# Keeping the pieces of the next batch's transform out of every third slot of a GEGLU block (batches 3 to 7)

## The chip, the cores and the metric

The kernel runs on one core of one Trainium2 chip. The metric is the time of one execution on the device in microseconds (us). The time before is 620.68 us, the median of six runs between 619.86 and 621.28 us.

## The reference, cut to what matters

```
x: (8, 3008, 256)                                  # batch, sequence, channels
X   = real(fft(fft(x, axis=1), axis=2))            # Fourier mixing
X   = X.reshape(24064, 256)
g   = X @ w_gate                                   # 256 -> 1536
val = X @ w_val                                    # 256 -> 1536
out = (gelu(g) * val) @ w_out                      # 1536 -> 256, float32
```

## The kernel before, in words

**The transform.** The Fourier transform of one batch is made of matmuls. GpSimd first folds the input (sums and differences of a row and its mirror, lines 221 to 229) into `eo`. Eight pieces `s1t` (line 546) then multiply it by a table `G` in two or three matmuls each, and ScalarE copies each result to `S_sb` (line 558). Two DMA writes (`z_write`, line 562) put `S_sb` into DRAM, one DMA (`z_read`, line 571) brings it back in another layout as `Z_sb`, 768 KB. Seven more pieces follow: `tp_row` (line 621), one matmul that makes a row which a DMA writes to DRAM at once, and `tp_e` and `tp_o` (line 584) for each of three groups, four matmuls of up to 128 columns each, copied by ScalarE into `E_sb` and `O_sb` (line 601). Last, `tp_rows` (line 638) is two DMAs that spread the row. The transform of the real input has a mirror symmetry, so only about half of the tokens is held, as an even part E and an odd part O. A token and its mirror come out of E plus O and E minus O.

**The feed-forward block.** Each batch has three chunks of 512, 512 and 481 columns of E and O, and each chunk has 12 slices of the 1536 hidden features. One slice of one chunk is a *slot*: 36 slots a batch, 288 in all, numbered here from 0. In slot i TensorE does the following, in this order (`feed`, lines 981 to 1000): the gate of slice i (two matmuls into a `ps_g` bank), the mirrored gate of slice i-1 (one more matmul into the bank of that slice), the first value matmul of slice i, four matmuls of the second layer, the second value matmul of slice i-1, four more matmuls of the second layer, and then whatever the table `fill` has for this slot. ScalarE applies gelu to the gate (line 690) and to the mirrored gate (line 699). VectorE does three operations a slot on the value (lines 718, 734, 736), GpSimd one (line 738). The second layer works on the chunk before.

**Evacuation.** The second layer sums 128 tokens and their mirrors in one `ps_o` bank over six pieces of four matmuls. With two pieces in a slot a bank is complete at the end of every third slot, the slots with number 2 modulo 3. There ScalarE copies it to `out_sb` (line 783), and four DMAs store it (line 668), issued by SyncE (SP).

**Buffers.** PSUM has two `ps_g` banks, three `ps_v`, one `ps_o` and two `ps_dft` for the transform pieces. A `ps_g` bank is filled at the start of slot i, gets its mirrored part in slot i+1, is released by that part's gelu (line 699), and is filled again at the start of slot i+2.

**The order.** Each engine runs its instructions in program order, and the program order is written by hand: `plan` (line 889) builds the tables `fill` (pieces, loads and DMAs of the transform) and `pool` (the folding on GpSimd), keyed by slot, and `feed` empties them slot by slot. The transform of batch b runs in the slots of batch b-1. Its `s1t` pieces begin up to nine slots ahead of that batch and are placed from line 949 on. The function `spread` (line 920) places the seven later pieces evenly between two slots, and `taken` holds the slots that it used. What `fill` has for a slot comes behind the slot's evacuation in program order, on SP too: the DMAs of a `fill` entry in a slot with an evacuation are issued after that evacuation's stores.

Of the kernel before, what the change touches and what calls it, by code (L numbers as in the profile page):

```python
# [18 lines left out]
def _sub(base: bass.AP, free_pattern, free_offset, part_start=0, part_num=None):  # L19
    p_step, p_count = base.ap[0]  # L20
    if part_num is None:
        part_num = p_count - part_start
    pat = [[p_step, part_num]] + [list(x) for x in free_pattern]
    off = base.offset + part_start * p_step + free_offset
    return ap_replace(base, ap=pat, offset=off)
# [3 lines left out]
def kernel(  # L29
# [80 lines left out]
    def S_tile():  # L110
        return work([96, 16, C], BF16, "A", 1, "S_sb")
# [33 lines left out]
    def psum(tag):  # L145
        bufs = {"g": 2, "v": 3, "o": 1, "dft": 2}[tag]
        return psum_pool.tile([128, 512], FP32, tag=tag, bufs=bufs, name=f"ps_{tag}")
# [287 lines left out]
    def load_wo(q):  # L435
        n = NFC // 2
        nc.gpsimd.dma_start(
            out=Wo_sb[:, q * n : (q + 1) * n, :],
            in_=ap_replace(
                moe_w_out, ap=[[C, 128], [128 * C, n], [1, C]], offset=moe_w_out.offset + q * n * 128 * C))  # L440
# [61 lines left out]
    def state(b):  # L502
        return dst_.setdefault(b, {})
# [20 lines left out]
    def ch(b, pp, engine="A", qs=(0, 1)):  # L524

        def run():
            st = state(b)
            A = st["A"]
            if "Z" not in st:
                st["Z"] = Z_tile()  # L530
            ps = ps_any(b)
            for i, q in enumerate(qs):
                k = 2 * (2 * pp + q)
                for g in range(2):
                    nc.tensor.matmul(  # L535
                        ps[:, i * C : (i + 1) * C], _sub(A, [[1, 128]], g * NK * K1 + k * K1), II[:, g, :, :],
                        start=g == 0, stop=g == 1)
            n = len(qs) * C
            dst = _sub(st["Z"], [[1, n]], pp * 512 + qs[0] * C)
            if engine == "A":  # L540
                nc.scalar.activation(dst, ps[:, :n], AF.Copy)
            else:
                nc.vector.tensor_copy(dst, ps[:, :n])
        return run

    def s1t(b, jg, half):

        def run():
            st = state(b)
            if "S" not in st:  # L550
                st["S"] = S_tile()
            ps = psum("dft")
            for q, js in enumerate(JG[jg][2 * half : 2 * half + 2]):
                for j in js:
                    nc.tensor.matmul(  # L555
                        ps[:96, q * C : (q + 1) * C], G[:, j, :], _sub(eo, [[1, C]], j * C),
                        start=(j == js[0]), stop=(j == js[-1]))
            nc.scalar.activation(  # L558
                _sub(st["S"], [[1, 512]], (4 * jg + 2 * half) * C, part_num=96), ps[:96, :], AF.Copy)
        return run  # L560
# [23 lines left out]
    def tp_e(b, gi, g=0, engine="A", tag=None):  # L584
        def run():
            st = state(b)
            if b not in EO_bufs:
                EO_bufs[b] = EO_tiles()
            ps = psum(tag) if tag else ps_any(b)
            for pair, o, n in pairs(gi):  # L590
                nc.tensor.matmul(  # L591
                    ps[:, o : o + n], st["Z"][:, pair, g * 128 : g * 128 + 128], _sub(TP, [[1, n]], g * 128),
                    start=True, stop=True)
            if b == 0 and g == 1:
                for pair, o, n in pairs(gi):
                    nc.tensor.matmul(
                        ps[0:1, o : o + n], st["Z"][:, pair, 128:129], _sub(TP, [[1, n]], 0), start=True, stop=True)
            n = chunk_len[gi]
            dst = _sub(EO_bufs[b][g], [[1, n]], chunk_off[gi])
            if engine == "A":  # L600
                nc.scalar.activation(dst, ps[:, :n], AF.Copy)  # L601
            else:
                nc.vector.tensor_copy(dst, ps[:, :n])
        return run
# [42 lines left out]
    def tp_o(b, gi, engine="A"):  # L647
        return tp_e(b, gi, 1, engine)
# [238 lines left out]
    NS = NG * NFC  # L887

    def plan():

        fill, pool = {}, {}

        def at(table, s, f):
            table.setdefault(s, []).append(f)

        early = []
        for gi in (1, 2):
            e = "A" if gi == 1 else "V"
            early += [ch(0, 2 * gi), ch(0, 2 * gi + 1, e), tp_e(0, gi), tp_o(0, gi, e), tp_y(0, gi)]
        for s, f in (  # L900
                (0, make_w(0, 256, 256, m_engine="P")), (0, make_w(1, 256, 256, engine="V", m_engine="P")),
                (1, make_w(1, 512, 512, (1,), m_engine="P")), (1, lambda: load_wo(0)), (1, lambda: load_wo(1)),
                (2, make_w(0, 512, 512, (0,), "V")), (3, make_w(0, 512, 512, (1,))), (3, make_w(1, 512, 512, (0,), "V")),
                (4, make_w(1, 1024, 512, (1,), "V")), (5, make_w(0, 1024, 512, (0,), "V")),
                (5, make_yw()), (6, make_w(0, 1024, 512, (1,))), (6, tp_y(0, 0)), (7, make_w(1, 1024, 512, (0,), "V"))):
            at(fill, s, f)
        for i, f in enumerate(early):
            at(fill, (7, 8, 9, 10, 11, 12, 13, 14, 15, 16)[i], f)


        at(fill, 7, lambda: nc.sync.dma_start(
            out=ap_replace(yrow_dram[0], ap=[[0, 1], [1, 64]]), in_=EB_bufs[0][0:1, 0:64]))
        for k, s in ((0, 8), (1, 9), (2, 9)):
            at(fill, s, lambda k=k: load_part(2, k, (load_forward,)))
        for k, s in ((0, 18), (1, 19), (2, 19)):
            at(fill, s, lambda k=k: load_part(2, k, (load_mirror,)))

        taken = set()

        def spread(b, s0, s1):  # L920

            items = [tp_row(b)] + [f(b, gi) for gi in range(NG) for f in (tp_e, tp_o)]
            for i, f in enumerate(items):
                s = s0 + (i * (s1 - s0) // (len(items) - 1) if b > 1 else (0, 2, 3, 6, 8, 11, 13)[i])
                at(fill, s, f)
                taken.add(s)
                if b == 1 and i and i % 2 == 0:
                    at(fill, s + 1, tp_rows(b, chunk_off[i // 2 - 1], chunk_len[i // 2 - 1]))
            if b > 1:
                at(fill, s + 1, tp_rows(b, 0, HALF))  # L930

        for b in range(1, B):
            s0 = (b - 1) * NS
            ops = []
            for j0, nj in PIECES:
                ops += fold_ops(b, j0, nj, nc.gpsimd)
            per = len(ops) // 5
            first, n = (s0 - 19, 30) if b == 3 else (s0 - 22, 32)
            slot_of = [first + i * n // len(ops) for i in range(len(ops))]
            if b == 2:  # L940
                slot_of = [26, 27, 29, 30, 31, 33, 34, 37, 38, 39, 41, 42, 43, 45, 46, 49, 50, 50, 51, 51]
            if b == 1:
                slot_of = [4, 4, 5, 5, 6, 6, 7, 7, 8, 8, 9, 13, 13, 14, 15, 15, 16, 17, 17, 18]
            for s, f in zip(slot_of, ops):
                at(pool, s, f)
            if 1 < b < B - 1:
                for k, piece in ((0, 1), (1, 3), (2, 4)):
                    at(fill, slot_of[piece * per + 1] + 1, lambda b=b, k=k: load_part(b + 1, k))
            s = s0 - 9 if b > 1 else 12
            for i, (jg, piece) in enumerate(((2, 1), (1, 2), (0, 3), (3, 4))):  # L950
                ready = slot_of[piece * per + per - 1] + 2
                for g in range(2):
                    s = max(s + 1, ready)
                    while s in taken:
                        s += 1
                    at(fill, s, s1t(b, jg, g))
                if i == 2:
                    at(fill, s + 1, z_write(b, 0, 12))
                if i == 3:
                    at(fill, s + 1, z_write(b, 12, 4))  # L960
            at(fill, s + 2, z_read(b))
            if b == 1:
                spread(b, s + 7, s + 20)
                continue
            assert s + 7 < s0 + NS - 10
            spread(b, s + 7, s0 + NS - 5 if b == 2 else s0 + NS - 6)
        return fill, pool

# [70 lines left out]
```

## Time and profile before

| what | value |
|---|---|
| median of six runs | 620.68 us |
| the profiled execution, its own time | 620.76 us |
| its span in the trace | 618.9 us |
| TensorE weight loads busy | 406.6 us (66%) |
| VectorE busy | 576.5 us (93%) |
| ScalarE busy | 425.1 us (69%) |
| GpSimd busy | 508.8 us (82%) |
| ScalarE gelu, line 690 / line 699 | 288 at 589 ns / 288 at 586 ns |
| ScalarE evacuation, line 783 | 92 at 598 ns |
| ScalarE copy of an `s1t` piece, line 558 | 56 at 589 ns |
| ScalarE copy of a `tp_e` or `tp_o` piece, line 601 | 45 at 588 to 589 ns |
| granted TensorE clock, mean | 0.997 |

[...]Two instructions that follow each other on one engine overlap by about 0.1 us in the records, so the spacing of their starts tells the cost in a busy queue better than the duration. The ends of matmuls are modelled, but their starts are recorded.

### The profile page before, as it was taken

To read this page: it belongs to the slowest core of one execution; us is meant where nothing else is said; L and a number is where in the kernel's file an instruction comes from. 1 tells how busy PE (TensorE), PEld (TensorE's weight loads), DVE (VectorE), ACT (ScalarE), POOL (GpSimd) and SP (SyncE) were. 2 spreads that over 40 slices of the span, in tenths; PEclk is the share of its full clock that TensorE was granted. 3 is DMA by queue.
4 is the path that set the end of the run, shared out by engine and by line. 5 is a ranking of instruction groups with operands and counts; after the bars stand their busy time and mean duration, and the time that the engine had idled before them with its cause. 6 is when DMAs were issued, how large, how long until landed. Compare 5 with 4: busy or idle time off the path is not lost.

```text
span 618.9 us, 12794 instructions
## 1 busy us (share of the span) xinstructions
PE 610.6 (99%) x4230; PEld 406.6 (66%) x4230; DVE 576.5 (93%) x940; ACT 425.1 (69%) x825; POOL 508.8 (82%) x513
## 2 busy tenths in 40 slices
PE   8999999999999999999999999999999999999997
PEld 4456666666666666666666666666666666666666
DVE  8789999999999999999999999999999999999992
ACT  6787677677766676666767677666776667666651
POOL 8889899999997999879997899969987555555561
PEclk8999999999999999999999999999999999999999
DMA  9961825546362364632553335543123322221123
GB/s 173 200 136 34 237 69 154 135 120 183 85 170 79 94 150 111 156 96 55 160 139 101 112 97 117 140 107 95 44 69 77 95 56 51 64 50 43 40 52 82
DMA packets 52466, 65.40 MB, mean 106 GB/s; under 512 B 7629, under 2 KB 47278, under 8 KB 50004
## 3 DMA queue, kind: packets, MB, share of 16 engines
q1 hardware_dynamic: 45472, 49.03, 30.4%
q0 software_dynamic: 6608, 15.29, 11.5%
q8 instruction: 33, 0.54, 0.4%
q10 hardware_dynamic: 320, 0.26, 0.2%
q14 instruction: 33, 0.27, 0.1%
HBM read 39.65 MB, written 30.17 MB: 113 GB/s over the span
## 4 chain that ended last, share of the span: by engine, by line
PE 95%; DMA 2%; DVE 1%; ACT 1%; issue 1%; POOL 0%; POOLq 0%; SPq 0%; ACTq 0%; DVEq 0%
PE ps_o L763 39%; PE ps_g L674 30%; PE ps_v L674 20%; PE ps_dft L555 2%; PE ps_dft L591 2%; DMA xb<-in_x_dram,idx 1%; DMA out_dram<-out_sb 1%; PE ps_dft L451 1%; PE ps_o L832 0%; ACT A_sb L519 0%; PE ps_dft L535 0%; DVE h_sb L730 0%; DVE W_sb L459 0%; POOLq L1034 0%; POOL h_sb L738 0%
## 5 line engine op out<-in xcount | busy, mean ns | idle before, releaser
L738 POOL TENSOR_TENSOR h_sb<-gelu_sb,v_sb 128x512 bf16<-128x512 bf16 (+1 forms) x280 | 319.7, 1146 | 90.8 <-DVE v_sb L736 77.4
L763 PE MATMUL ps_o<-Wo_sb,h_sb 128*128 128x256 bf16 (+1 forms) x2232 | 334.5, 273 | 0.0
L763 PEld LDWEIGHTS <-h_sb 128*128 128x128 bf16 (+1 forms) x2304 | 228.7, 100 | 111.1 <-POOL h_sb L738 1.2
L690 ACT ACTIVATE gelu_sb<-ps_g 128x512 bf16<-128x512 f32 (+1 forms) x288 | 169.5, 589 | 99.3 <-PE ps_g L674 93.1
L718 DVE SCALAR_TENSOR_TENSOR ve_sb<-EB_sb,yw,ps_v 128x512 f32<-128x512 bf16 (+1 forms) x280 | 206.2, 737 | 20.6 <-PE ps_v L674 16.6
L674 PEld LDWEIGHTS <-W_sb 128*128 128x128 bf16 x1440 | 138.1, 98 | 81.2 <-issue 3.6
L734 DVE TENSOR_TENSOR h_sb<-gelu_sb,ps_v 128x512 bf16<-128x512 bf16 (+1 forms) x280 | 189.8, 678 | 1.4 <-ACT gelu_sb L699 1.0
L736 DVE SCALAR_TENSOR_TENSOR v_sb<-ve_sb,ps_v 128x512 f32<-128x512 f32 (+1 forms) x280 | 187.4, 669 | 0.0
L674 PE MATMUL ps_g<-O_sb,W_sb 128*128 128x512 bf16 (+1 forms) x576 | 168.9, 374 | 0.1
L699 ACT ACTIVATE gelu_sb<-ps_g 128x512 bf16<-128x512 f32 (+1 forms) x288 | 168.8, 586 | 0.0
L674 PE MATMUL ps_v<-E_sb,W_sb 128*128 128x512 bf16 (+1 forms) x288 | 108.0, 375 | 0.7 <-DVE W_sb L459 0.6
L674 PE MATMUL ps_g<-E_sb,W_sb 128*128 128x512 bf16 (+1 forms) x288 | 108.0, 375 | 0.7 <-ACT gelu_sb L699 0.3
L674 PE MATMUL ps_v<-O_sb,W_sb 128*128 128x512 bf16 (+1 forms) x288 | 108.0, 375 | 0.0
L783 ACT ACTIVATE out_sb<-ps_o 128x512 f32<-128x512 f32 x92 | 55.0, 598 | 34.3 <-PE ps_o L763 34.0
L229 POOL TENSOR_TENSOR eo_sb<-ab_sb 94x512 bf16<-94x512 f32 (+1 forms) x70 | 77.7, 1111 | 0.4
L558 ACT ACTIVATE S_sb<-ps_dft 96x512 bf16<-96x512 f32 x56 | 33.0, 589 | 18.7 <-PE ps_dft L555 18.2
L225 POOL TENSOR_TENSOR ab_sb<-x_raw,x_raw 94x508 f32<-94x508 f32 (+1 forms) x30 | 33.0, 1099 | 0.0
L222 POOL TENSOR_TENSOR ab_sb<-x_raw,x_raw 94x508 f32<-94x508 f32 (+1 forms) x30 | 33.0, 1099 | 0.0
L555 PE MATMUL ps_dft<-eo_sb,G 94*96 94x256 bf16 x119 | 22.3, 272 | 0.0
L601 ACT ACTIVATE E_sb<-ps_dft 128x512 bf16<-128x512 f32 (+1 forms) x23 | 13.5, 588 | 8.9 <-PE ps_dft L591 8.9
L163 POOL DMA_INDIRECT x_raw<-in_x_dram,idx x18 | 17.2, 957 | 2.9 <-issue 0.8
L601 ACT ACTIVATE O_sb<-ps_dft 128x512 bf16<-128x512 f32 (+1 forms) x22 | 13.0, 589 | 7.5 <-PE ps_dft L591 7.0
(151 smaller groups left out, 208.2 us busy)
## 6 DMA issues: line engine op xcount, KB each, us to landing
out_dram<-out_sb SPq DMA_DIRECT2D x364, 64.0 KB
x_raw<-in_x_dram SPq DMA_DIRECT2D x10, 768.0 KB
Z_sb<-z SPq DMA_DIRECT2D x7, 768.0 KB
z<-S_sb SPq DMA_DIRECT2D x7, 576.0 KB
EB_sb<-yrow SPq DMA_DIRECT2D x6, 376.2 KB
z<-S_sb SPq DMA_DIRECT2D x7, 192.0 KB
x_raw<-in_x_dram SPq DMA_DIRECT2D x2, 640.0 KB
x_stage<-in_x_dram SPq DMA_DIRECT2D x1, 768.0 KB
```

Source lines behind the costliest of these rows:

```text
L222: eng.tensor_tensor(ab(0, 1, up), fwd(1, up), mir(255, down), op=ALU.add)
L229: eng.tensor_tensor(_sub(eo, [[C, nj], [1, 128]], j0 * C + g * 128), ab(0, 0, [[1, 128]]), ab(1, 0, [[1, 128]]), op=op)
L555: nc.tensor.matmul(ps[:96, q * C : (q + 1) * C], G[:, j, :], _sub(eo, [[1, C]], j * C), start=(j == js[0]), stop=(j == js[-1]))
L674: nc.tensor.matmul(ps[:, :n], W[nm, part][:, fs], src, start=start, stop=stop, **kw)
L690: nc.scalar.activation(gl[:, 0, :n], pg[:, :n], AF.Gelu)
L699: nc.scalar.activation(_sub(gl, [[-1, n]], TOK + n - 1), pg[:, :n], AF.Gelu)
L718: nc.vector.scalar_tensor_tensor(ve[:, :n], EB_bufs[b][:, c0 : c0 + n], yw[:, fc : fc + 1], pv[:, :n], op0=ALU.mult, op1=ALU.add)
L734: nc.vector.tensor_tensor(st["h"][:, fc, 0, :n], gl[:, 0, :n], pv[:, :n], op=ALU.mult)
L736: nc.vector.scalar_tensor_tensor(_sub(vv, [[-1, n]], n - 1), ve[:, :n], 2.0, pv[:, :n], op0=ALU.mult, op1=ALU.subtract)
L738: nc.gpsimd.tensor_tensor(st["h"][:, fc, 1, :n], gl[:, 1, :n], vv[:, :n], op=ALU.mult)
L763: nc.tensor.matmul(pso[:m, half], st["h"][:, fc, sign, h0 : h0 + m], Wo_sb[:, fc, :], start=(fc == 0 and not (first and sign)), stop=(fc = ...
L783: nc.scalar.activation(_sub(osb, [[1, 2 * C]], 0, part_num=m), pso[:m, :], AF.Copy)
```

## The change

A new function `quiet` moves a slot number up until the slot has no transform piece yet and isn't 2 modulo 3. From batch 3 on it places all pieces: the eight `s1t`, and the seven of `spread`, which no longer spaces them evenly but takes the next such slot for each. Batches 1 and 2 keep their places. What is placed relative to a piece (`z_write`, `z_read`, `tp_rows`) goes with it. The bound of the assertion is eased by two slots.

```diff
         taken = set()
 
+        def quiet(s):
+
+            while s in taken or s % 3 == 2:
+                s += 1
+            taken.add(s)
+            return s
+
         def spread(b, s0, s1):
 
             items = [tp_row(b)] + [f(b, gi) for gi in range(NG) for f in (tp_e, tp_o)]
             for i, f in enumerate(items):
-                s = s0 + (i * (s1 - s0) // (len(items) - 1) if b > 1 else (0, 2, 3, 6, 8, 11, 13)[i])
+                if b > 2:
+                    s0 = s = quiet(s0)
+                else:
+                    s = s0 + (i * (s1 - s0) // (len(items) - 1) if b > 1 else (0, 2, 3, 6, 8, 11, 13)[i])
                 at(fill, s, f)
                 taken.add(s)
...
                 for g in range(2):
                     s = max(s + 1, ready)
-                    while s in taken:
+                    while b == 2 and s in taken:
                         s += 1
+                    s = quiet(s) if b > 2 else s
                     at(fill, s, s1t(b, jg, g))
...
-            assert s + 7 < s0 + NS - 10
+            assert s + 7 < s0 + NS - 8
             spread(b, s + 7, s0 + NS - 5 if b == 2 else s0 + NS - 6)
```

Worked out from the code, the pieces of batch 4 and of the start of batch 5 stand in these slots (batches 5 to 7 are like them, 36 slots apart; an E marks a slot with an evacuation):

| piece | before | after |
|---|---|---|
| `s1t` 1 to 4 of batch 4 | 101E, 103, 105, 106 | 103, 105, 106, 108 |
| `s1t` 5, 6; first `z_write` | 112, 113E; 114 | 112, 114; 115 |
| `s1t` 7, 8; second `z_write` | 118, 119E; 120 | 118, 120; 121 |
| `z_read` | 121 | 122E |
| `tp_row` | 126 | 127 |
| `tp_e`, `tp_o` in turn | 128E, 130, 132, 134E, 136, 138 | 129, 130, 132, 133, 135, 136 |
| `tp_rows` | 139 | 137E |
| `s1t` 1 to 4 of batch 5 | 137E, 139, 141, 142 | 138, 139, 141, 142 |

## The prediction

> **What bounds the kernel now.** I read the busy shares first, then the chain that ended last, then the waits.
>
> ```profile
> PE 610.6 (99%) x4230; PEld 406.6 (66%) x4230; DVE 576.5 (93%) x940; ACT 425.1 (69%) x825; POOL 508.8 (82%) x513
> PE 95%; DMA 2%; DVE 1%; ACT 1%; issue 1%; POOL 0%; POOLq 0%; SPq 0%; ACTq 0%; DVEq 0%
> ```
>
> TensorE is busy for 99% and makes 95% of the chain. The ends of matmuls are modelled, so 99% could hide small waits. I therefore measured slots in the timeline, from the start of a slot's first gate matmul to the next slot's. Slots without a transform piece take 1.95 us with chunks of 512 (316.03 to 317.98) and 1.89 us with 481 (306.07 to 307.96). A 512-column matmul starts 0.21 to 0.22 us before its follower, a 256-column one 0.11 us: 5 x 0.215 + 8 x 0.11 = 1.95. So the plain slot is nothing but matmuls. VectorE, at 93%, isn't the bound: its line 718 starts 0.40 to 0.42 us behind its value matmul in nearly every slot, so it follows and has no backlog.
>
> The list of waits from 36 to 600 us (total, times, longest) shows what TensorE's weight loads still wait for; the middle line, left out here, is one wait of the opening:
>
> ```profile
> PEld L674 <- issue: 2.1, 13, 0.2
> ...
> PEld L763 <- POOL h_sb L738: 0.7, 3, 0.2
> ```
>
> The timeline (start, duration, engine, line, operation) around 283 us, slots 128 and 129, shows where the first kind comes from:
>
> ```profile
> 281.05 0.38 PE L674 MATMUL ps_g<-E_sb,W_sb 128*128 128x512 bf16 x1
> ...
> 281.74 0.60 ACT L690 ACTIVATE gelu_sb<-ps_g 128x512 bf16<-128x512 f32 x1 [0.87 <-PE ps_g L674]
> ...
> 282.23 0.59 ACT L699 ACTIVATE gelu_sb<-ps_g 128x512 bf16<-128x512 f32 x1
> ...
> 283.20 0.60 ACT L783 ACTIVATE out_sb<-ps_o 128x512 f32<-128x512 f32 x1 [0.38 <-PE ps_o L763]
> 283.22 0.38 PE L674 MATMUL ps_g<-E_sb,W_sb 128*128 128x512 bf16 x1
> ...
> 283.69 0.59 ACT L601 ACTIVATE E_sb<-ps_dft 128x512 bf16<-128x512 f32 x1
> ...
> 284.17 0.60 ACT L690 ACTIVATE gelu_sb<-ps_g 128x512 bf16<-128x512 f32 x1
> ...
> 284.65 0.62 ACT L699 ACTIVATE gelu_sb<-ps_g 128x512 bf16<-128x512 f32 x1
> ...
> 285.32 0.38 PE L674 MATMUL ps_g<-E_sb,W_sb 128*128 128x512 bf16 x1
> 285.32 0.53 PEld L674 LDWEIGHTS <-W_sb 128*128 128x128 bf16 x3 [0.15 <-issue]
> ```
>
> Slot 128 (from 281.05) has an evacuation and a transform piece. Both copies land at the start of slot 129 (from 283.22), one behind the other: 283.20, 283.69. The gelus follow at the same spacing of 0.48 us, and the mirrored gelu ends at 284.65 + 0.62 = 285.27. It is what releases the `ps_g` bank, and the next gate starts 0.05 us later. In slot 128 the gelu waits for its gate and ends at 282.23 + 0.59 = 282.82, 1.77 us into the slot, against 2.05 in slot 129. A plain slot needs the bank at 1.95, so it has 0.13 us to spare. Two copies ahead of the gelus overdraw that; one does not, since slot 137 with one copy (299.94) ends its mirrored gelu at 301.44, 1.70 us in.
>
> **What the change removes.** Before, 26 of the 75 pieces of batches 3 to 7 stand in evacuation slots; after, none. The wait shows only where the slot behind has no piece of its own, as a piece's 0.2 us of matmuls hides it. Read from the starts of gates, with a gap of 0.05 to 0.06 us behind the mirrored gelu in each:
>
> - Behind the first `tp_e` (slots 93, 129, 165, 201, 237): 2.09 to 2.10 for 1.95, 5 x 0.15 = 0.75 us.
> - Behind `tp_o` of the second group (99, 135, 171, 207, 243): 2.04 for 1.89, 5 x 0.15 = 0.75 us.
> - Behind the sixth `s1t` (114, 150, 186, 222): 2.08 for 1.95, 4 x 0.13 = 0.52 us.
> - Behind the eighth (120, 156, 192, 228): 1.98 for 1.95, 4 x 0.03 = 0.12 us.
>
> Together 2.14 us. One more may go: in slot 110 the weight load waits 0.21 us for GpSimd's product (it reads "POOL h_sb L738"), which makes the slot 0.11 us longer. The `s1t` that moves from 106 to 108 gives GpSimd 0.215 us more before it. Between 0 and 0.11 us; I take 0.1, since GpSimd was waiting for VectorE at 241.88, one slot earlier, so it has no older backlog to carry. The same wait in slots 146 and 182 stays: no piece between 141 and it moves. **Sum: 2.2 us.**
>
> **What it moves, and what that costs.** Counts of matmuls and copies stay.
>
> - *Matmuls and copies.* Pieces now stand in neighbouring slots (132 and 133, 135 and 136). Each slot then sees one copy at its start, the case of slot 137 above, and the second `ps_dft` bank takes the second piece. Cost 0. If the cover failed (a copy and an evacuation at one start), it would be the 0.15 us again.
> - *Stores.* They wait for evacuations, which no longer have copies right behind them. Cost 0.
> - *The second `z_write` and `z_read`.* This is the risky part: SP issues in order. In batches 4 to 7 `z_read` moves from slot 121 to 122 and so behind that slot's four stores; the list of SP's instructions confirms it. Before:
>
> ```profile
> 268.03 0.34 SPq L566 DMA_DIRECT2D z<-S_sb  x1
> 271.26 0.35 SPq L577 DMA_DIRECT2D Z_sb<-z  x1
> 272.01 9.09 SPq L668 DMA_DIRECT2D out_dram<-out_sb  x8
> 281.20 0.79 SPq L633 DMA_DIRECT2D yrow<-yrow_sb  x1
> ```
>
> Four stores take SP 2.4 us (302.45, 2.38), so the read goes out near 272.0 + 2.4 = 274.4. By the DMA shares per microsecond, the transfers of 271.26 are over by 276.0 (0.65 busy in the microsecond before, 0.00 in the next): at most 4.74 us. So it lands by 279.2. `tp_row`, one slot later than before, needs it at the end of slot 127, near 281.0. Spare: 1.8 us, cost 0. The narrowest case of the trace had 4.5 us (74.32 to `tp_row` at 78.81) with stores beside it, and TensorE didn't wait. In batch 3 each write moves behind four stores. The second goes out when those of slot 86 end, at 198.59 + 2.41 = 201.0, the read 3.2 us later (268.03 to 271.26), and it lands 4.74 after that, at 209.0; `tp_row` needs it at the end of slot 93, near 211.7. Without this cover every microsecond of lateness stops TensorE for a microsecond in each batch.
> - *`tp_row`'s own DMA and `tp_rows`.* The first is one slot later. The second, in 137, is issued behind that slot's stores, as it was from 139 (304.94, right behind stores that end at 304.83). The next batch uses it from slot 144, at 316.0. Cost 0.
> - *Loads, GpSimd's folding.* Not moved; a piece only ever moves later than its fold.
>
> **Two rules against this sum.** ScalarE is the least busy engine, at 69%. The Trainium skill (Perfetto Trace Analysis, Identifying the Most-Contended Engine) says to improve the engine with the highest occupancy first. By it, relieving ScalarE brings nothing: 620.7 us. The rows say otherwise: ScalarE's average leaves 31% free, but its three or four instructions in one slot's order set the start of the bound engine. I take the rows. Second, TensorE: Matmul & The Clock Gate (Back-to-back issue gap) gives about 131 ns per 512-column matmul in a sustained stream. By that, TensorE would have 5 x 0.084 = 0.42 us of air in a slot, which would swallow a wait of 0.15: gain 0. Here back-to-back starts are 215 ns apart and nothing is waited for, so each 0.15 counts in full.
>
> **Rivals.**
>
> - *A second limit takes the place of the wait.* With ScalarE early, the same slots could hang on GpSimd's product, as in slots 110, 146 and 182. For it: GpSimd is at 82%, with folds in the same stretch. Against: it caught up soon after the stalls, waiting 0.46 us for VectorE at 286.44 and 0.64 at 309.16. If more than half of the gain went so, 619.5 to 620.9.
> - *`z_read` comes too late: slower.* It decides once the read needs over 6.6 us from 274.4. The trace has one case of 4.74 with stores beside it. At 7.6 us TensorE stops 1 us in each of batches 4 to 7: 620.7 - 2.2 + 4 = 622.5.
> - *The change doesn't do what it says.* `tp_rows` and `z_read` do stand in evacuation slots now, but neither has a copy on ScalarE; no piece is left there. I fold this into the first rival.
>
> **How the numbers follow.** The profiled execution took 620.76, which becomes 618.56. The median of the runs is 620.68, 0.08 lower, so I predict 618.5. Its own range is 617.7 to 619.4: the waits that I leave in place (one of 0.17 in slot 152, two for GpSimd) may move either way. Chances: forecast 0.79, second limit 0.13, late read 0.08. For 8 in 10 the range goes from 617.7 up to 620.1, into the second limit. A difference under 0.2%, 1.24 us, can't be told from none; faster begins below 619.44. The second limit is mostly no change: faster 0.80, same 0.12, slower 0.08.
>
> **What would show it.** Right: slots 129, 135, 150 and their like at 1.95 or 1.89; ten of the 13 waits under "issue" gone; mirrored gelus ending 1.7 to 1.8 us into every slot; `Z_sb` read near 274 and no wait before line 627. Wrong: the same slots still long with another releaser, or a gap before line 627.

## The result and the profile after

The changed kernel takes 619.36 us (median of 17 runs, 617.83 to 620.24) where the kernel before takes 620.77 us (38 runs). The ratio is 0.9975 with a 95% interval of 0.9968 to 0.9981, so it is 1.2 to 2.0 us faster; 618.5 us was forecast.

The page of the profile after begins with the busy times:

```profile
span 616.3 us, 12792 instructions
PE 607.1 (98%) x4230; PEld 405.8 (66%) x4230; DVE 575.8 (93%) x940; ACT 425.3 (69%) x825; POOL 508.4 (82%) x513
```

The span is 2.6 us shorter than that of before, which is more than the change did. The slots begin at 17.40 us instead of 18.53, so 1.13 us of it lie in the opening, which is the same in both kernels; in its first 20 us the granted TensorE clock was 1.00 here and 0.91 before. For this reason I compare one stretch in all traces, from the first gate of slot 68 to the first gate of slot 254. It holds all pieces of batches 3 to 7, with equal work in both kernels. Before it runs from 159.00 to 537.45, 378.45 us; after it runs from 158.22 to 534.84, 376.62 us. That is **1.83 us less**.

The waits of TensorE's weight loads from 36 to 600 us (total, times, longest) were 2.1 us in 13 and 0.7 us in 3. Now they are:

```profile
PEld L674 <- issue: 0.7, 3, 0.4
PEld L763 <- POOL h_sb L738: 0.4, 2, 0.2
```

The ten waits of 0.15 to 0.16 us are gone, and so is one of GpSimd's three, in slot 110. (The shortest wait in these lists is 0.15 us; those of slots 114 and 120 and their like are shorter and stand in neither.) The timeline after of slot 130, the one behind the first `tp_e` of batch 4, shows a single copy ahead of the gelus:

```profile
283.90 0.38 PE L674 MATMUL ps_g<-E_sb,W_sb 128*128 128x512 bf16 x1
...
284.10 0.60 ACT L601 ACTIVATE E_sb<-ps_dft 128x512 bf16<-128x512 f32 x1 [0.60 <-PE ps_dft L591]
...
284.60 0.59 ACT L690 ACTIVATE gelu_sb<-ps_g 128x512 bf16<-128x512 f32 x1
...
285.09 0.59 ACT L699 ACTIVATE gelu_sb<-ps_g 128x512 bf16<-128x512 f32 x1
...
286.08 0.38 PE L674 MATMUL ps_g<-E_sb,W_sb 128*128 128x512 bf16 x1
```

The mirrored gelu ends at 285.68, 1.78 us into the slot, and the next gate at 286.08 comes 0.40 us later. Nothing waits: the slot is 1.95 us and one piece long. In the slots from 72 to 251 every mirrored gelu now ends 1.70 to 1.78 us into its slot, but for slot 152 (2.06). Before, 25 of them, those behind a piece in an evacuation slot, ended at 1.92 to 2.04. So the waits are really gone and not just hidden behind the moved pieces.

SP's queue after (first column the issue) has the read of Z behind four stores, as worked out:

```profile
270.74 2.41 SPq L668 DMA_DIRECT2D out_dram<-out_sb  x4
273.25 0.52 SPq L577 DMA_DIRECT2D Z_sb<-z  x1
276.59 3.11 SPq L668 DMA_DIRECT2D out_dram<-out_sb  x4
280.27 0.78 SPq L633 DMA_DIRECT2D yrow<-yrow_sb  x1
```

`tp_row` runs at 279.68, 6.43 us behind the read's issue, without a wait.

**What came in place of it.** In slot 135 a new wait of 0.03 us appears. Lines of the timeline after, then before:

```profile
294.19 0.37 PE L674 MATMUL ps_g<-E_sb,W_sb 128*128 128x481 bf16 x1
...
294.39 0.60 ACT L783 ACTIVATE out_sb<-ps_o 128x512 f32<-128x512 f32 x1 [0.37 <-PE ps_o L763]
...
295.04 0.60 PE L763 MATMUL ps_o<-Wo_sb,h_sb 128*128 128x256 bf16 x4
```

```profile
295.58 0.60 ACT L783 ACTIVATE out_sb<-ps_o 128x512 f32<-128x512 f32 x1 [0.39 <-PE ps_o L763]
295.60 0.37 PE L674 MATMUL ps_g<-E_sb,W_sb 128*128 128x481 bf16 x1
...
296.42 0.60 PE L763 MATMUL ps_o<-Wo_sb,h_sb 128*128 128x256 bf16 x4
```

After, the evacuation ends at 294.99, and the first matmul of the second layer, which refills the only `ps_o` bank, starts 0.05 us later, 0.85 us into the slot. Before, the same evacuation began ahead of the slot's gate, since a piece's matmuls lay between, and this matmul started 0.82 us in. With the piece gone from the evacuation slot the evacuation comes 0.22 us later against the gate, and in chunks of 481 columns that is just too late. (In chunks of 512 this matmul starts 0.86 us in anyway.) There are 15 slots of this kind, behind an evacuation and in the third chunk, between slots 72 and 251. In the changed kernel this matmul starts 0.85 us in in all of them. Before, it did so in six, whose evacuation slots had no piece, and at 0.81 in the other nine. The new wait is thus 9 x 0.035 = 0.31 us.

### The profile page after: what moved, and what is told of

It is laid out like the page before. It is cut to its first block, busy times and chain, and to the rows that moved or that the text cites. A ratio compares the mean times of both kernels' runs of the same rounds, so it can differ in the third digit from the quotient of the medians.

```text
span 616.3 us, 12792 instructions
## 1 busy us (share of the span) xinstructions
PE 607.1 (98%) x4230; PEld 405.8 (66%) x4230; DVE 575.8 (93%) x940; ACT 425.3 (69%) x825; POOL 508.4 (82%) x513
## 4 chain that ended last, share of the span: by engine, by line
PE 93%; ACT 2%; DVE 2%; DMA 1%; issue 1%; SPq 1%; DVEq 0%; ACTq 0%; POOL 0%; POOLq 0%
PE ps_o L763 39%; PE ps_g L674 29%; PE ps_v L674 20%; PE ps_dft L555 2%; PE ps_dft L591 2%; DMA out_dram<-out_sb 1%; PE ps_dft L451 0%; SPq L668 0%; ACT A_sb L519 0%; DMA O_sb<-yrow 0%; DVE h_sb L730 0%; PE ps_dft L535 0%; DVE W_sb L459 0%; ACT G L351 0%; ACT L426 0%
```

## The experiments

Theory: ScalarE takes its work in order, and two copies ahead of a slot's gelus keep the `ps_g` bank from TensorE for 0.13 to 0.15 us. Rivals: the gain comes from where the pieces stand on TensorE or SP; ScalarE's load matters and not its order; and, for the forecast, that the later read of Z was close to costing more than the change brings. "Stretch" is the one from slot 68 to slot 254, from one trace of each kernel; ratios are of timed runs, with the interval.

**The changed kernel again**, twice:

> The changed kernel once more, beside the three variants on the same chip. If the waits for the gate's bank were the whole difference, it is 1.8 us faster than the kernel before (the slots from 68 to 253 became 1.83 us shorter in its trace), and slots 24 to 67, which the change doesn't touch and which were 0.34 us longer there, come out the same as before but for chance.

> The changed kernel a third time, beside the combined version on the same chip: 1.4 to 1.8 us faster than the kernel before; slots 68 to 253 in its trace again 1.83 us shorter than before.

| run | ratio to before | stretch less before |
|---|---|---|
| on record | 0.9975 (0.9968 to 0.9981) | -1.83 |
| again | 0.9977 (0.9969 to 0.9984) | -1.83 |
| third | 0.9970 (0.9957 to 0.9983) | -1.71 |

The stretch repeats within 0.12 us, and the 0.12 is one slot, 72. Slots 24 to 67 took 89.72 us before and 90.06, 89.69 and 90.02 in these three, so their 0.34 us was chance. It sits in two slots. In slot 28 `tp_row` of batch 1 comes only 4.4 to 5.3 us behind the issue of its read of Z, and waits for it in some traces: the slot is 0.09 us longer than before in the run on record and 0.26 in the third. Slot 36 is 0.30 us longer in the run on record. There the first matmul that reads `O_sb` is late, and it starts 2.56 us behind the issue of the DMA that writes the row into `O_sb` (89.79 to 92.35); in slot 72 of the third run it is 2.61 us (164.86 to 167.47). That fits a wait for this DMA, though the profile names no releaser for it.

**The `s1t` pieces alone, and the later pieces alone.** The first leaves `spread` as it was, the second the placing of `s1t`:

```diff
-                if b > 2:
-                    s0 = s = quiet(s0)
-                else:
-                    s = s0 + (i * (s1 - s0) ...
+                s = s0 + (i * (s1 - s0) ...
```

```diff
-                    while b == 2 and s in taken:
+                    while s in taken:
                         s += 1
-                    s = quiet(s) if b > 2 else s
```

> Only the s1t pieces keep out of the evacuation slots; the seven later pieces are spread as before. Theory (two ScalarE copies ahead of the gelus hold the ps_g bank): only the slots behind the sixth and eighth s1t, 114 and 120 and their like, and slot 110 lose their wait: 4 x 0.125 + 4 x 0.02 + 0.11 + 0.06 in slot 72, 0.7 to 0.8 us faster than before; slots 129 and 135 and their like stay at 2.10 and 2.04 us. Rival (it is the closer packing and the earlier end of the later pieces that pays): no gain, since these are as before.

> Only the seven later pieces keep out of the evacuation slots; the s1t pieces stand as before, one or two slots later only where a piece is in the way. Theory: slots 129 and 135 and their like lose their wait, 5 x 0.13 + 5 x 0.11, less 0.03 in one or two slots a batch that newly wait for the ps_o bank: 1.0 to 1.2 us faster than before; slots 114, 150, 186, 222 stay at 2.08 us. Rival (the gain is the s1t pieces' distance from GpSimd's folds): about 0.

The `s1t` pieces alone: ratio 0.9987 (0.9977 to 0.9996), stretch -0.79 us, as expected. Slots 114, 150, 186 and 222 lose their wait, and 129 and 135 and their like keep it, except slot 93, into which batch 3's `tp_e` has moved. Not expected: the waits for GpSimd in slots 146 and 182 go too, because an `s1t` piece is pushed from 142 to 144, and batch 3 gets a new wait of 0.13 us in slot 96, where an `o1` in 95 has an evacuation and no piece behind it.

The later pieces alone: ratio 0.9997 (0.9988 to 1.0006), no difference that the times can tell, and stretch -0.77 us where 1.0 to 1.2 were expected. All ten waits at 93, 99, 129, 135 and their like go, down to the 0.03 us for `ps_o` in 99, 135 and theirs. But slots 138, 174 and 210 newly wait 0.14 us. The evacuation slots 137, 173 and 209 hold an `s1t`, as they did before; there a `tp_o` in 138 and its like hid the wait, and that piece has moved. My count had missed that a wait hidden behind a piece comes out when the piece leaves. Slot 239 is 0.16 us longer for a reason that stays open: its gate's gelu starts 0.28 us late, though ScalarE is idle just ahead of it. Slot 152 has the same, 0.16 us, in every kernel here but the two with extra copies below; the prediction left it in place. The two halves add to 1.56, the whole brings 1.83: each half exposes waits that the other removes.

**Only the order on ScalarE.** The kernel before, with every piece in its old slot; in an evacuation slot the copy (lines 558 and 601 of before) is kept back:

```diff
+            if b > 2 and slot[0] % 3 == 2:
+                late.append(copy)
+            else:
+                copy()
...
             if before:
                 before[0]["g"][before[1]]()
+            while late:
+                late.pop(0)()
+            slot[0] = i
```

> The pieces of the kernel before, all in their old slots; only where a piece of batches 3 to 7 stands in an evacuation slot, its ScalarE copy comes behind the two gelus of the next slot instead of ahead of them. TensorE's and SP's orders are those of before. Theory: the order on ScalarE is the whole cause, so the waits in slots 93, 99, 114, 120, 129, 135 and their like go: 2.1 us faster than before, at least as good as the change, as the evacuation still starts early and ps_o is free in time. Rival (moving the pieces on TensorE or the reads on SP is what pays): no gain.

Ratio 0.9971 (0.9961 to 0.9982), stretch -2.06 us. Its timeline around slot 135 (lines shifted by the edit: 608 is the copy, 701 and 710 the gelus, 794 the evacuation):

```profile
295.14 0.60 ACT L794 ACTIVATE out_sb<-ps_o 128x512 f32<-128x512 f32 x1 [0.39 <-PE ps_o L774]
295.16 0.37 PE L685 MATMUL ps_g<-E_sb,W_sb 128*128 128x481 bf16 x1
...
295.83 0.57 ACT L701 ACTIVATE gelu_sb<-ps_g 128x481 bf16<-128x481 f32 x1
...
296.30 0.57 ACT L710 ACTIVATE gelu_sb<-ps_g 128x481 bf16<-128x481 f32 x1
...
296.75 0.60 ACT L608 ACTIVATE O_sb<-ps_dft 128x512 bf16<-128x512 f32 x1
...
297.05 0.37 PE L685 MATMUL ps_g<-E_sb,W_sb 128*128 128x481 bf16 x1
```

The copy is behind the gelus, the next gate comes 1.89 us after this slot's, and no wait is left in any of the 18 slots of the prediction's four kinds: they became 2.04 us shorter, and slot 72 0.06. GpSimd's waits in 110, 146 and 182 stay, 0.21 us each. TensorE's and SP's orders are those of before, so they aren't where the gain comes from. In the nine slots that newly wait for `ps_o` in the changed kernel, the first matmul of the second layer starts 0.81 us in here, as before. So this kernel has 0.31 us over the changed one there, and lacks the 0.11 of slot 110. Their times don't tell the two apart.

**ScalarE's load against its order.** The changed kernel with 60 more copies of `W_sb` into a scratch tile, `extra`, once ahead of and once behind the gelus:

```diff
                     store(b, ci, sub, 1, osb[:, 1, :], nc.sync)
+                    if 72 <= 36 * b + 12 * (ci + 1) < 252:
+                        for _ in range(1):
+                            nc.scalar.activation(extra[:, :], W_sb[:, 0, 0:512], AF.Copy)
```

```diff
                 before[0]["g"][before[1]]()
+                if 72 <= i < 252 and i % 3 == 0:
+                    nc.scalar.activation(extra[:, :], W_sb[:, 0, 0:512], AF.Copy)
```

> The changed kernel with one more ScalarE copy (128 x 512, from the weights into a scratch tile that nobody reads) right behind each of the 60 evacuations between slots 71 and 251, so ahead of the next slot's gelus. Theory: the mirrored gelu then ends about 2.25 us into the slot; the next gate waits 0.36 us where the slot has no piece (25 slots) and 0.14 us where it has one (35): 14 us slower than the changed kernel, near 633 us. Rival (ScalarE is busy 69% and has air for it): no slower.

> The same 60 extra copies, each placed behind the two gelus of the same slot instead of ahead of them. ScalarE's busy time grows as much as with the copies ahead. Theory: only what stands ahead of the mirrored gelu counts, so within 0.5 us of the changed kernel, 619 us. Rival (ScalarE's load counts): as slow as with the copies ahead.

Ahead: 632.81 us, ratio 1.0211 (1.0192 to 1.0230), stretch 391.18 us, 14.56 more than the changed kernel. The copies stand ahead of the gelus of slots 75, 78 and so on to 252. Of these, 26 have no piece (the expectation counted 25) and became 0.39 us longer on average; the 34 with one became 0.15 us longer. Behind: 617.77 us, ratio 0.9964 (0.9950 to 0.9977), stretch 376.46 us, 0.16 less than the changed kernel, which is slot 152's wait. The same 60 instructions, and all of the cost is in their place. The largest group of the weight loads' waits from 100 to 600 us is the first line with the copies ahead and the second with the copies behind. There it is the only group, and none under "issue" is left:

```profile
PEld L675 <- issue: 13.0, 41, 0.4
```

```profile
PEld L764 <- POOL h_sb L739: 0.7, 3, 0.3
```

**The late read of Z, made to happen.** The changed kernel with one shift:

```diff
-            at(fill, s + 2, z_read(b))
+            at(fill, s + 5 if b > 3 else s + 2, z_read(b))
```

> The changed kernel with the read of Z in batches 4 to 7 three slots later, so behind one more group of four stores, as the slower rival has it. By the trace of the changed kernel those stores end at 279.7 and tp_row needs Z at 279.7. The read then goes out near 279.8 and lands within 4.7 us: TensorE stands still at tp_row for 4 to 4.7 us in each of four batches, 16 to 19 us slower than the changed kernel, near 636 us. If the read is quicker than the 4.74 us taken as its upper bound, less; at 3 us it is 12 us slower. In the changed kernel itself no wait is expected at tp_row, as its read goes out at 273.25.

It takes 646.97 us, ratio 1.0413 (1.0387 to 1.0440); its stretch is 27.8 us longer than the changed kernel's, 6.0 to 7.9 us a batch where 4 to 4.7 were expected. In batch 4 the read goes out at 281.66. TensorE's timeline:

```profile
281.23 0.60 PE L763 MATMUL ps_o<-Wo_sb,h_sb 128*128 128x256 bf16 x4
286.20 0.41 PE L627 MATMUL ps_dft<-TP,Z_sb 128*89 128x128 bf16 x1 [4.36 <-DMA Z_sb<-z]
286.40 0.63 PE L674 MATMUL ps_g<-E_sb,W_sb 128*128 128x512 bf16 x1
286.83 1.06 PE L674 MATMUL ps_g<-O_sb,W_sb 128*128 128x512 bf16 x2
287.68 0.63 PE L674 MATMUL ps_v<-E_sb,W_sb 128*128 128x512 bf16 x1
288.11 1.06 PE L763 MATMUL ps_o<-Wo_sb,h_sb 128*128 128x256 bf16 x4
```

From issue to use it is 4.54 us here and 4.73, 4.55 and 4.70 in the other three batches, so 4.74 was the right size. The slot with `tp_row` is 4.6 to 5.1 us longer in each batch, which is the waiting. What comes on top is in the starts behind it: 286.40, 286.83, 287.68 are 0.43 us for each 512-column matmul instead of 0.215. The rows by stretch have the granted clock ahead of the last two columns:

```profile
282.00:286.00 4.00, 0.00 (x0) 0.00 (x0) 0.79 (x2) 0.00 (x0) 3.57 (x4) 0.97 0.69 213
286.00:289.00 3.00, 2.80 (x10) 1.42 (x11) 0.65 (x1) 1.36 (x3) 0.00 (x0) 0.50 0.01 1
289.00:290.00 1.00, 1.00 (x7) 0.65 (x7) 0.53 (x2) 0.06 (x1) 0.00 (x0) 0.90 0.00 0
```

In batches 5 and 7 the clock stays low longer, as in this row of batch 5, whose `tp_row` runs at 365.62:

```profile
368.00:371.50 3.50, 3.28 (x14) 1.80 (x14) 1.85 (x4) 1.34 (x4) 0.94 (x1) 0.55 0.00 0
```

After 4.6 to 5.1 us without matmuls the clock is at half, for 3.4 us in batches 4 and 6 and 6.8 us in 5 and 7, by the clock's own records in the trace. The slots behind `tp_row` are 1.4, 2.6, 1.7 and 2.8 us longer in the four batches. The Trainium skill (TensorE: Matmul & The Clock Gate, What's actually happening) says that the clock drops to half after an idle window of about 3.4 us and returns after a busy one of about the same length. Batches 4 and 6 agree. In 5 and 7 a first such window begins with 1.3 and 1.0 us of standstill left, and the clock returns after a second one. A short stop costs no more than itself: in slot 28 of two other traces the wait for Z was 0.28 and 0.70 us (third run and copies behind), and the slot 0.26 and 0.69 us longer than before.

**The two remedies together**: `s1t` as in the change, the later pieces spread as before, copies in evacuation slots kept back from batch 2 on.

> The s1t pieces placed as in the change, the later pieces spread as before, and the copy of each piece that still stands in an evacuation slot, from batch 2 on, moved behind the next slot's gelus. Theory: no wait behind ScalarE's copies is left, GpSimd's waits in slots 110, 146 and 182 go as they did with the s1t pieces alone, and no slot newly waits for ps_o: 2.2 to 2.4 us faster than before, 0.3 to 0.5 us faster than the change. If something else holds TensorE as soon as these are gone, no faster than the change.

> The combined version (s1t pieces as in the change, later pieces spread as before, copies of pieces in evacuation slots behind the next gelus) once more, beside the changed kernel. Its slots 68 to 253 were 2.22 us shorter than before and 0.39 us shorter than the changed kernel's. If that is real it comes out 2.0 to 2.4 us faster than before; the 0.39 us over the change are within what two sets of runs can tell apart only just.

Ratios 0.9962 (0.9949 to 0.9976) and 0.9969 (0.9961 to 0.9977), stretches -2.22 and -2.09 us. In the first trace its weight loads have left, from 36 to 600 us and besides one wait of the opening (1.1 us), only:

```profile
PEld L685 <- issue: 0.3, 2, 0.2
```

In the second trace slots 36 and 72 add 0.57 and 0.27 us, at the same matmul as in the changed kernel's traces above. Against the expectation, slots 102, 138, 174 and 210 newly wait 0.03 us for `ps_o`, since the `s1t` pieces have left the evacuation slots ahead of them.

It beats the kernel before. Over the changed kernel it is 0.39 us better in the stretch (against the run on record) and 0.38 (against the third), but the intervals of their timed ratios overlap, so the times don't show a gain there.

## Why the prediction was right

- **What bounds the kernel** (TensorE's stream, with ScalarE's order deciding a few starts): shown by the late copies, which change nothing but ScalarE's order, and by the 60 copies that cost 14.6 us ahead of the gelus and nothing behind them. The rule of the Trainium skill to treat the busiest engine first (Perfetto Trace Analysis, Identifying the Most-Contended Engine) would have put both at nothing.
- **The four kinds of slots.** Measured in the changed kernel against before, with the moved pieces' own matmuls taken off: behind the first `tp_e` 0.70 us of the 0.75, behind the sixth `s1t` 0.51 of 0.52, behind the eighth 0.08 of 0.12, slot 110 0.11 for 0.1. Each is within some hundredths a slot.
- **The signs.** The mirrored gelus end where the prediction said. Slots 129, 135 and 150 are not at 1.95 or 1.89 us, as it wrote, but at 2.18, 2.13 and 2.17: the pieces have moved into just these slots, as the table of slots ahead of the prediction shows and its list of signs forgot.
- **The term that was off:** behind `tp_o` of the second group, 0.59 us instead of 0.75. There the new wait for `ps_o`, 0.03 to 0.04 us a slot, takes part of the gain, and with slots 102, 138, 174 and 210 it amounts to 0.31 us. The prediction said of the stores that they cost nothing since they wait for evacuations; it didn't ask when the evacuation itself would start. A piece's matmuls behind a completed bank had been giving the evacuation a head start of 0.22 us. So 2.2 became 1.83 us in the stretch and 1.2 to 2.0 in the times: the mechanism held, and the forecast of 2.2 itself was too high. Of the 1.83, 0.06 are luck: slot 72 belongs to none of the prediction's kinds, and in the third run it was 0.07 us longer than before instead.
- **No cost on SP.** Right, with the spare of 1.8 us: 6.43 us from issue to `tp_row`, and 4.54 to 4.73 us needed. The rival's price, a microsecond for each one of lateness, held for the two short stops in slot 28. At stops of 4.6 to 5.1 us it was too low by 1.4 to 2.8 us a batch, as the clock wasn't counted.
- **A second limit behind ScalarE**: the one that the rival named, GpSimd's product, isn't seen; its waits in 146 and 182 stayed at 0.21 and 0.22 us. A second limit that nobody named, the `ps_o` bank, took the 0.31 us.
- **Back-to-back rate.** The 131 ns for a 512-column matmul that the Trainium skill gives (TensorE: Matmul & The Clock Gate, Back-to-back issue gap) doesn't hold here. The late copies gave back 2.04 us of the 2.14 counted, which they couldn't had TensorE had air.

## What to carry to other kernels

On an engine that works in order, look at what stands ahead of the instruction that frees the bottleneck's buffer, not at how busy the engine is: here 60 copies cost 14.6 us in one place and nothing a microsecond later. Before moving work away from a slot, ask what it hid (a wait of its predecessor) and what it gave a head start to (an evacuation), since both come back. Here it was enough to reorder the slack engine, with the bottleneck's order and the DMA queue left as they were.

## What the runs showed of the hardware that was not expected

A long standstill costs TensorE more than itself, a short one doesn't. After a wait of 4.6 to 5.1 us for a DMA the granted clock was 0.50 for 3.4 or 6.8 us, and a late read cost 6.0 to 7.9 us a batch; waits of 0.28 and 0.70 us cost 0.26 and 0.69.

The clock in the opening differs from run to run too. In four of the twelve profiles here it was 1.00 over the first 20 us, and the slots began at 17.33 to 17.80 us; in the other eight it was lower, mostly 0.91, and they began at 17.75 to 19.52. How much of that is the clock's doing wasn't tested. The difference of 1.13 us between before and after is over half of what this change is worth, so spans of single traces can't be compared for it.
